# A gated recurrence and an ELU layer in one kernel: every engine's queue in a written-out order, and 53 products of zeros in place of 20

## The chip, the cores and the metric

The kernel runs on one core of a Trainium2 chip. The core has five engines with a queue each: TensorE (PE in the profile, its weight loads PEld), VectorE (DVE), ScalarE (ACT), GpSimd (POOL) and SyncE (SP, which here only issues DMAs). An engine works through its queue in order and waits on semaphores for the others. The metric is the device time in microseconds, the median of several runs.

## The reference, cut to what matters

```
sig = 1 / (1 + exp(-f_logit));  f = lower_bound + (1 - lower_bound) * sig     # (2, 6080, 256)
h[t] = f[t] * h[t-1] + (1 - f[t]) * x[t]                                      # a scan over 6080 steps
h1 = h.reshape(12160, 256) @ w_in                                             # w_in 256 x 2048
g  = where(h1 > 0, h1, exp(min(h1, 0)) - 1)                                   # ELU
out = g @ w_out                                                               # w_out 2048 x 256
```

All values are 32-bit floats.

## The kernel before, in words

The 6080 steps are cut into 12 pages (`SIZES`: 512, 448, then ten of 512). A page holds four tiles y of 128 channels by 512 steps: two halves of the channels (k) for two batches (t). The 2048 hidden columns are cut into eight quads of 2 x 128 columns, so the kernel runs through 96 quads (`NQ`).

To keep the precision, an operand is split into a high part that TensorE's fast format holds and the low rest, and a product becomes three: high by high, low by high, high by low. ScalarE's copy makes the high part, a subtraction on VectorE or POOL the low one (`operand`, `halves`, `split`). Only the first quad (`NATIVE = 1`) multiplies in plain 32-bit floats, which needs no splitting; each of its products takes four passes. The first 12 quads (`plain_quad`) multiply directly; later ones (`quad`) use seven products of sums and differences in place of eight (M1 to M7), and one quad a page from page 3 on is "wide" and does the same for the second matrix.

The weights come as 64-bit floats and are cut down to 32 bits on the chip: `conv` is an Abs on ScalarE (L855), a clamp (L903 on VectorE, L910 on POOL), a mask (L916) and two merging steps (L924). The scan of a page is `chain`: for each batch t, a tanh on ScalarE over f (L855), a scaling of it by the per-channel constants fa and fb (L851), a fused step on VectorE that forms (f - 1) * x (L1068) and the scan itself on VectorE (L1077). fa and fb are made on VectorE (L1464) from `lower_bound`, which ScalarE's queue loads by a DMA (L1460). The ELU of a tile is an exponential and a ReLU on ScalarE (L855) and a VectorE step (L1189). The second matrix's products (L1236) add up in PSUM; at the end of a page they are copied out and stored.

Ahead of the first real product TensorE runs products of a zero tile by itself (`idle`, L1448, 256 columns each). They write a PSUM tile that nobody reads.

No loop issues these instructions. Every operation is put into a plan, `Plan.add(engine, cost, want, fn, reads, writes, ...)`, and gets the next number. `Plan.order()` then simulates the engines with the given costs, always takes the operation that can start first (among near ties the one with the lowest `want`), and returns the order in which the program issues them. `SHIFT` moves the `want`, the earliest start or the patience of single operations. An operation with `other` may go to POOL in place of VectorE or the other way round, and products of zeros are dropped when they find no room (`latest`). Instructions of VectorE that touch SBUF alone (`lock`) and all of POOL's are chained: where two neighbours in the issued order are on different engines, the second waits for the first.

The numbers of the first operations, counted along the calls, are used below: 0 the zero tile's memset (POOL), 1 to 60 the products of zeros, 61 the load of `lower_bound`, 62 and 63 fb and fa, 64 to 71 the eight loads of page 0 (for t, for k: f then x, 256 KB each), 72 to 74 the first weight tile in three parts, 75 to 79 and 80 to 84 the `conv` of its parts 0 and 1, 85 to 92 the `chain` of t=0 (tanh 85, 86; scaling 87, 88; fused step 89, 90; scan 91, 92), 93 to 100 that of t=1 in the same way, 101 to 105 the `conv` of part 2. Of the later ones: 121 to 124 are the second weight tile's conv, 130 and 131 the high and the low half of it, 111 the low part of one y, 204, 210, 216 and 222 the last ELU step of the first quad's four tiles.

In the old order TensorE's queue begins with 19 products of zeros and has a 20th behind the first quad's second product. ScalarE's queue begins 61, 75, 80, 85, 87, 93; VectorE's 62, 63, 76, 77, 78, 79, 81, 82, 83, 84, 89, 91, 97, 99, 98, 102, 100, 103, 104, 90, 105, 92, 210, 222, 121; SP's 72, 73, 64, 71, 68, 65, 69, 70, 74.

Of the kernel before, what the change touches and what calls it, by code (L numbers as in the profile page):

```python
# [13 lines left out]
B, S, D, DFF = 2, 6080, 256, 2048  # L14
# [48 lines left out]
SHIFT = {  # L63
# [513 lines left out]
def stage(p):  # L577

    return str(p) if p <= WIDE_FROM else "e" if p == NP - 1 else "s"
# [1029 lines left out]
```

## Time and profile before

| | |
|---|---|
| time, median of 3 runs | 996.96 us (995.84 to 997.40) |
| span of the profiled execution | 995.6 us |
| its own time | not listed apart from the span; the median lies 1.4 us above it |
| TensorE | busy 984.9 us, 99% |
| weight loads | 813.9 us, 82% |
| VectorE | 763.5 us, 77% |
| ScalarE | 806.0 us, 81% |
| POOL | 423.3 us, 43% |
| DMA | 46.5 MB, 47 GB/s over the span |

A row of a timeline names its start, its duration, the engine, the line of the program, the operation, what it writes and reads and how many were merged; in square brackets stands the time for which the engine was idle before it, and what ended that. Ends of matmuls are modelled and overlap the next start.

### The profile page before, as it was taken

What the parts mean: (1) busy time and instruction counts of PE and PEld (TensorE: products, weight loads), DVE (VectorE), ACT (ScalarE), POOL (GpSimd) and SP (SyncE); (2) the same over time, 40 slices, a digit from 0 to 9 for tenths busy, and PEclk for the clock granted to TensorE, in tenths of its full rate; (3) what the DMA queues carried; (4) which work ended last, traced back from release to release, by engine and by line L of the source; (5) the groups of instructions that cost most, each with busy time, mean ns of one, the idle gap of its engine ahead of it and who ended that gap; (6) DMA issues with size and microseconds to landing.
All of it is one profiled execution on the core that took longest, in us unless ns stands there. A gap on an engine that the chain in (4) does not pass through costs nothing.

```text
span 995.6 us, 11936 instructions
## 1 busy us (share of the span) xinstructions
PE 984.9 (99%) x4333; PEld 813.9 (82%) x4333; DVE 763.5 (77%) x1005; ACT 806.0 (81%) x1138; POOL 423.3 (43%) x260
## 2 busy tenths in 40 slices
PE   7999999999999999999999999999999999999998
PEld 4788899888888878888888888888888888888886
DVE  7989788887888588687778678768868767867665
ACT  6899787976898698888879779878888887977764
POOL 0221414345525735634632742661563463274422
PEclk8999999999999999999999999999999999999999
DMA  6331121000020030010101102102001010100101
GB/s 211 128 122 38 69 101 43 37 1 1 22 106 1 1 126 8 36 67 18 43 23 62 43 1 85 43 1 86 5 38 64 23 43 20 66 0 1 43 1 43
DMA packets 10427, 46.51 MB, mean 47 GB/s; under 512 B 1280, under 2 KB 1280, under 8 KB 7808
## 3 DMA queue, kind: packets, MB, share of 16 engines
q1 hardware_dynamic: 10224, 45.75, 12.6%
q8 instruction: 34, 0.56, 0.2%
q14 instruction: 25, 0.20, 0.1%
q10 hardware_dynamic: 144, 0.00, 0.0%
HBM read 33.29 MB, written 12.45 MB: 46 GB/s over the span
## 4 chain that ended last, share of the span: by engine, by line
PE 97%; ACT 1%; DVE 1%; DMA 0%; issue 0%; SPq 0%; DVEq 0%
PE o L1236 51%; PE hv L1149 17%; PE hz L1149 17%; PE hx L1149 6%; DMA gh<-fx 0%; ACT e L855 0%; PE h(_188 L1134 0%; PE h(_205 L1134 0%; PE h(_195 L1134 0%; PE h(_202 L1134 0%; PE h(_263 L1149 0%; DVE v L924 0%; PE h(_304 L1149 0%; PE h(_336 L1149 0%; PE h(_350 L1149 0%
## 5 line engine op out<-in xcount | busy, mean ns | idle before, releaser
L838 POOL TENSOR_TENSOR gl<-hs,gh 128x1024 fp32r<-128x1024 f32 (+1 forms) x71 | 170.0, 2396 | 263.3 <-DVE y L1077 83.5
L855 ACT ACTIVATE e<-e 128x512 f32<-128x512 f32 (+3 forms) x278 | 208.0, 756 | 6.2
L1236 PE MATMUL o<-gh,woL 128*128 128x512 f32 (+1 forms) x706 | 208.9, 387 | 0.0
L1236 PE MATMUL o<-gl,woH 128*128 128x512 f32 (+1 forms) x706 | 204.8, 387 | 0.0
L1236 PE MATMUL o<-gh,woH 128*128 128x512 f32 (+1 forms) x706 | 204.3, 387 | 0.1
L1149 PE MATMUL hv<-yo,wiH 128*128 128x512 f32 (+1 forms) x504 | 190.0, 388 | 0.0
L1149 PE MATMUL hz<-yo,wiH 128*128 128x512 f32 (+1 forms) x504 | 188.8, 388 | 0.0
L1236 PEld LDWEIGHTS o<-gh,woH 128*128 128x128 f32 x706 | 132.4, 188 | 26.5 <-DVE v L838 0.5
L1236 PEld LDWEIGHTS o<-gh,woL 128*128 128x128 f32 x706 | 132.5, 188 | 26.4 <-ACT gh L849 0.3
L1236 PEld LDWEIGHTS o<-gl,woH 128*128 128x128 f32 x706 | 132.5, 188 | 26.2
L849 ACT CAST gh<-hs 128x1024 fp32r<-128x1024 f32 (+1 forms) x95 | 98.7, 1040 | 30.8 <-PE o L1236 22.6
L1189 DVE SCALAR_TENSOR_TENSOR hs<-hs,e 128x1024 f32<-128x1024 f32 (+1 forms) x84 | 101.9, 1213 | 20.0 <-POOL yo L838 9.3
L1149 PEld LDWEIGHTS hv<-yo,wiH 128*128 128x128 f32 x504 | 94.6, 188 | 19.8
L1149 PEld LDWEIGHTS hz<-yo,wiH 128*128 128x128 f32 x504 | 94.6, 188 | 19.4
L849 ACT CAST gh<-g 128x1024 fp32r<-128x1024 f32 (+1 forms) x80 | 83.2, 1040 | 26.3 <-DVE g L1189 18.1
L838 POOL TENSOR_TENSOR ys<-y 128x512 f32<-128x512 f32 (+1 forms) x52 | 66.7, 1292 | 77.3 <-DVE y L1077 36.1
L1149 PE MATMUL hz<-yo,wiL 128*128 128x512 f32 (+1 forms) x252 | 97.8, 388 | 0.0
L1149 PE MATMUL hv<-yo,wiL 128*128 128x512 f32 (+1 forms) x252 | 97.8, 388 | 0.0
L855 ACT ACTIVATE e<-hs 128x1024 f32<-128x1024 f32 (+1 forms) x84 | 88.5, 1054 | 11.4 <-DVE hs L838 9.2
L838 DVE TENSOR_TENSOR q<-q,hv 128x512 f32<-128x512 f32 (+1 forms) x84 | 57.0, 679 | 43.8 <-PE hv L1149 36.8
L838 DVE TENSOR_TENSOR gl<-g,gh 128x1024 fp32r<-128x1024 f32 (+1 forms) x58 | 70.2, 1210 | 24.9 <-POOL ys L838 8.8
L838 DVE TENSOR_TENSOR hs<-q,hv 128x512 f32<-128x512 f32 (+1 forms) x84 | 57.3, 682 | 32.0 <-PE hv L1149 25.2
(380 smaller groups left out, 1596.2 us busy)
## 6 DMA issues: line engine op xcount, KB each, us to landing
raw<-fx SPq DMA_DIRECT2D x20, 1024.0 KB, 4.6
out_t<-v SPq DMA_DIRECT2D x22, 512.0 KB, 2.9
raw<-w SPq DMA_DIRECT2D x15, 512.0 KB, 4.6
raw<-fx SPq DMA_DIRECT2D x2, 896.0 KB, 4.3
gh<-fx SPq DMA_DIRECT2D x4, 256.0 KB, 6.1
gl<-fx SPq DMA_DIRECT2D x4, 256.0 KB, 4.9
out_t<-v SPq DMA_DIRECT2D x2, 448.0 KB, 2.5
raw<-w SPq DMA_DIRECT2D x2, 256.0 KB, 3.1
```

The costliest lines, as they stand in the source:

```text
L838: return e, cost, lambda: engines[e].tensor_tensor(out=out_(), in0=in0(), in1=in1(), op=op)
L849: nc.scalar.copy(out=out_(), in_=in_())
L855: nc.scalar.activation(out=out_(), in_=in_(), func=func, **args)
L1149: nc.tensor.matmul(out=hb(q, b), lhsT=(wiH if m == "h" else wiL)[:, i, wi], rhs=T[kind, p, name], start=(start and j == 0), stop=(j == len ...
L1189: lambda: nc.vector.scalar_tensor_tensor(out=gt(), in0=src(), scalar=0.0, in1=et(), op0=ALU.max, op1=ALU.subtract,), reads=src_names + [e] ...
L1236: nc.tensor.matmul(out=accs[p, e, t], lhsT=lhsT, rhs=rhs, start=(c == 1), stop=(c == total(p, e, t)), skip_group_check=True,)
```

## The change

`SHIFT` goes, and with it the planner's simulation. In its place stands `ORDER`, a string of 4408 tokens: the numbers of the operations in the order in which they are issued. A `~` behind a number takes the operation's other engine.

```diff
-SHIFT = {
-    '00.L00.0': 6.99, '00.L01.0': 0.21, '00.L10.0': -3.16, '00.L11.0': 5.87, '00.M00.0': -0.25,
...
+ORDER = (
+    " 73 0 31 7 80 26 61 72 64 14 81 75 30 62 82 63 68 65 76 83 85 77 87 93 95 84 78 79 70 69 74 71"
+    " 94 96 89 91 6 40 97 99 17 12 3 28 1 8 25 29 50 23 21 38 18 16 27 101 4 48 43 9 19 5 66 67 13"
+    " 20 47 44 22 51 86 88 49 52 114 98 102 100 118 33 53 42 15 32 39 36 24 45 34 37 2 120 112 35"
+    " 90 103 46 11 10 212 200 41 92 119 104 206 218 207 208 209 219 220 221 210 105 121 122 222 110"
+    " 106 123 124 135 134 201 213 214 211 111 223 130 215 131 108 202 216 107 113 109 136 203 137"
...
+    " 4403 4404 4405 4409 4334 4406 4393 4407 4410 4408 4411 4413 4412 4414"
+)
     def order(self):
...
+        order, done = [], set()
+        for token in ORDER.split():
+            i = int(token.rstrip("~"))
+            o = self.ops[i]
+            assert o["deps"] <= done and i not in done
+            if token.endswith("~"):
+                o.update(eng=o["other"][0], cost=o["other"][1], fn=o["other"][2], lock=True)
+            order.append(i)
+            done.add(i)
+        assert all(i in done or o["spare"] for i, o in enumerate(self.ops))
+        return order
```

Only the order within each engine's queue, and between VectorE's and POOL's locked instructions, has an effect. Read by engine, the new queues begin:

- TensorE: 52 products of zeros, 212, 200 (the two products of the first y), one product of zeros, 206, 218 (second y), 207, 219 (third), 201, 213 (fourth), 211, 223.
- ScalarE: 80, 61, 75, 85, 87, 93, 95, 94, 96, 101, 86, 88, 114, 120.
- VectorE: 81, 62, 82, 63, 76, 83, 77, 84, 78, 79, 89, 91, 97, 99, 98, 102, 100, 90, 103, 92, 104, 210, 105, 121, 122, 222, 123, 124, 111, 131.
- SP: 73, 72, 64, 68, 65, 70, 69, 74, 71, 66, 67.

All 4355 real operations are in both orders. 127 of them change between VectorE and POOL: of the splits of hs 71 are on POOL before and 43 after, of the weight sums 12 before and 34 after. Each of the 12 pages has an order of its own; before, pages 4 to 10 shared one set of shifts. The costs in `act_cost`, `pool_cost`, `pe_cost` and of the loads and scans change too, but nothing reads them any more.

## Rows read from the trace of the kernel before

**Rows 1.** The page, part 1: busy us (share of span) and instructions by engine.
```profile
PE 984.9 (99%) x4333; PEld 813.9 (82%) x4333; DVE 763.5 (77%) x1005; ACT 806.0 (81%) x1138; POOL 423.3 (43%) x260
```
**Rows 2.** Windows of the start: length, busy us by engine, granted clock, DMA, GB/s.
```profile
8.00:9.00 1.00, 0.00 (x0) 0.00 (x0) 0.90 (x2) 0.75 (x1) 0.00 (x0) 0.88 1.05 373
...
15.00:16.00 1.00, 1.00 (x2) 0.30 (x2) 0.57 (x1) 0.91 (x2) 0.00 (x0) 0.70 0.00 0
```
**Rows 3.** Windows by stage, same columns (PE, PEld, DVE, ACT, POOL).
```profile
25.00:45.00 20.00, 20.00 (x81) 14.93 (x81) 18.82 (x26) 17.78 (x29) 4.53 (x4) 1.00 0.36 112
45.00:340.00 295.00, 295.00 (x1341) 251.47 (x1340) 237.46 (x333) 243.24 (x367) 119.98 (x83) 1.00 0.13 49
...
345.00:371.00 26.00, 25.77 (x111) 20.34 (x110) 21.32 (x29) 23.60 (x33) 9.63 (x4) 1.00 0.33 122
```
**Rows 4.** Waits of TensorE's weight loads: us in total, times, longest.
```profile
PEld o L1236 <- ACT raw L849: 0.6, 1, 0.6
...
PEld o L1236 <- ACT v L849: 0.2, 1, 0.2
```
**Rows 5.** Timeline of the first 25 us, all engines.
```profile
0.73 0.41 ACTq L1460 DMA_DIRECT2D lb_sb<-lb  x1
...
1.20 4.36 PE L1448 MATMUL hzeros<-zeros 128*128 128x256 f32 x19 [1.20 <-POOL zeros L1439]
...
3.71 0.43 ACT L855 ACTIVATE v<-raw 128x256 f32<-128x256 f32 x1 [1.26 <-DMA raw<-w]
3.94 0.17 DVE L1464 TENSOR_SCALAR fb<-lb_sb 128x2 f32<-128x2 f32 x1 [3.94 <-DMA lb_sb<-lb]
4.01 0.16 DVE L1464 TENSOR_SCALAR fa<-lb_sb 128x2 f32<-128x2 f32 x1
4.26 0.29 DVE L903 TENSOR_SCALAR v<-v 128x256 f32<-128x256 f32 x1
...
6.37 0.88 DVE L924 SCALAR_TENSOR_TENSOR v<-raw,v 128x256 int32<-128x256 int32 x2
...
8.06 0.69 DVE L1068 SCALAR_TENSOR_TENSOR gh<-gh 128x512 f32<-128x512 f32 x1 [0.81 <-DMA gh<-fx]
8.79 1.23 DVE L1077 TENSOR_TENSOR_SCAN y<-gh 128x512 f32<-128x512 f32 x1
...
10.16 2.04 PE L1134 MATMUL h(_188<-y,v 128*128 128x512 f32 x2 [4.60 <-DVE y L1077]
...
15.43 0.69 DVE L1068 SCALAR_TENSOR_TENSOR gh<-gh 128x512 f32<-128x512 f32 x1 [0.47 <-ACT gh L851]
...
16.64 1.22 DVE L1077 TENSOR_TENSOR_SCAN y<-gh 128x512 f32<-128x512 f32 x1
...
18.19 1.02 PE L1134 MATMUL h(_188<-y,v 128*128 128x512 f32 x2
...
18.82 0.69 DVE L1189 SCALAR_TENSOR_TENSOR g<-h(_205,e 128x512 f32<-128x512 f32 x1 [0.96 <-ACT e L855]
...
19.05 1.02 PE L1134 MATMUL h(_195<-y,v 128*128 128x512 f32 x2
...
24.77 0.50 PE L1149 MATMUL h(_263<-yo,wiL 128*128 128x512 f32 x1 [0.42 <-DVE wiL L838]
```
**Rows 6.** DMA issues: count, KB each, us from issue to landing (second row: 3.5 to 4.0).
```profile
lb_sb<-lb ACTq DMA_DIRECT2D x1, 1.0 KB, 3.2
...
gl<-fx SPq DMA_DIRECT2D x2, 256.0 KB, 5.3
...
out_t<-v SPq DMA_DIRECT2D x2, 448.0 KB, 2.5
```
**Rows 7.** Groups by line and form, POOL and VectorE: busy us, mean ns.
```profile
L838 POOL TENSOR_TENSOR gl<-hs,gh 128x1024 fp32r<-128x1024 f32 x67 | 161.5, 2411 | 251.4 <-DVE y L1077 83.5 <-ACT gh L849 52.1 <-DVE raw L838 34.1
...
L838 DVE TENSOR_TENSOR gl<-hs,gh 128x1024 fp32r<-128x1024 f32 x20 | 24.4, 1219 | 1.6 <-ACT gh L849 1.6
```
**Rows 8.** Timeline of the tail.
```profile
991.50 0.58 ACT L849 COPY v<-o 128x512 f32<-128x512 f32 x1 [4.64 <-PE o L1236]
```

More of the change, by code (lines that the diff above doesn't have):

```diff
@@ L60 @@
 COPIES = {"M2": 2, "M5": 3}
-SHIFT = {
[510 rows of a table removed]
-}
+ORDER = (
[232 rows of a table added]
+)
 def stage(p):
-    return str(p) if p <= WIDE_FROM else "e" if p == NP - 1 else "s"
+    return "abcdefghijkl"[p]
 def wide(q):
@@ L593 @@
 class Plan:
-    LAG = 0.12
-    PATIENCE = 0.155
-    DRAIN = 0.17
-    TIE = 0.05
-    LINED = ()
     def __init__(self, pools):
@@ L645, in add @@
         deps.discard(i)
-        used = set(reads) | set(writes) | set(adds)
         self.ops.append(dict(
-            eng=eng, cost=cost, want=want + SHIFT.get(key, 0.0), fn=fn, key=key, deps=deps, used=used, takes=list(takes),
-            lock=lock, soonest=max(soonest, self.gate) + SHIFT.get(key + "@", 0.0),
-            latest=latest, other=other, patience=self.PATIENCE + SHIFT.get(key + "~", 0.0),
+            eng=eng, cost=cost, want=want, fn=fn, key=key, deps=deps, takes=list(takes), lock=lock,
@@ L651, in add @@
+            soonest=max(soonest, self.gate), spare=latest is not None, other=other,
         ))
     def order(self):
-        ops = self.ops
-        n = len(ops)
-        after = [[] for _ in range(n)]
-        missing = [len(o["deps"]) for o in ops]
-        for i, o in enumerate(ops):
-            for d in o["deps"]:
-                after[d].append(i)
-        users = {}
-        home = {}
-        for o in ops:
-            for pool, name in o["takes"]:
-                home[name] = pool
@@ L666, in order @@
-        for i, o in enumerate(ops):
-            for b in o["used"]:
-                if b in home:
-                    users[b] = users.get(b, 0) + 1
-        slots = {p: [0.0] * k for p, k in self.pools.items()}
-        asks = {}
-        for o in ops:
-            if o["latest"] is None:
-                for name in [name for pool, name in o["takes"] if pool in self.LINED]:
-                    asks[name] = min(asks.get(name, float("inf")), o["want"])
-        lines = {p: [] for p in self.pools}
@@ L678, in order @@
-        for name in sorted(asks, key=asks.get):
-            lines[home[name]].append(name)
-        for p in lines:
-            lines[p].reverse()
-        held, ends = set(), {}
-        ready = [o["soonest"] for o in ops]
-        def engines(o):
-            return [o["eng"], o["other"][0]] if o["other"] else [o["eng"]]
-        waiting = {}
-        for i, o in enumerate(ops):
-            for e in engines(o):
-                waiting.setdefault(e, set())
-                if not missing[i]:
-                    waiting[e].add(i)
@@ L694, in order @@
-        free = {e: 0.0 for e in waiting}
-        locked, holder = 0.0, None
-        dropped = set()
-        start = [0.0] * n
-        done = [0.0] * n
-        left = n
-        while left:
-            best = None
-            for e, mine in waiting.items():
-                for i in [
-                    i for i in mine
-                    if ops[i]["latest"] is not None and max(ready[i], free[e]) > ops[i]["latest"]
-                ]:
-                    mine.discard(i)
-                    dropped.add(i)
-                    left -= 1
-                able = []
-                for i in mine:
-                    o = ops[i]
-                    t = asked = max(ready[i] + (o["patience"] if e != o["eng"] else 0.0), free[e])
-                    lock = o["lock"] or e == "POOL"
-                    if lock:
-                        t = max(t, locked + (self.LAG if e != holder else 0.0))
-                    for pool, name in o["takes"]:
-                        if name not in held:
-                            turn = name not in asks or lines[pool][-1] == name
-                            t = max(t, min(slots[pool])) if slots[pool] and turn else float("inf")
-                    if t < float("inf"):
-                        able.append((t, o["want"], i, asked if lock else t))
-                if not able:
-                    continue
-                first = min(able)[0]
-                pick = min((k for k in able if k[0] < first + self.TIE), key=lambda k: k[1:3])
-                if (best is None or (pick[0], pick[3]) < (best[0], best[3])):
-                    best = (*pick, e)
-            if best is None:
-                break
-            t, _, i, _, e = best
-            o = ops[i]
-            if e != o["eng"]:
-                o.update(eng=e, cost=o["other"][1], fn=o["other"][2], lock=True)
-            for pool, name in o["takes"]:
-                if name not in held:
-                    slots[pool].remove(min(slots[pool]))
-                    held.add(name)
-                    if name in asks:
-                        lines[pool].pop()
-            start[i] = t
-            free[e] = t + o["cost"]
-            done[i] = t + o["cost"] + (self.DRAIN if e == "PE" else 2.8 if e == "SP" else 0.0)
-            if o["lock"] or e == "POOL":
-                locked, holder = t + o["cost"], e
-            for mine in waiting.values():
-                mine.discard(i)
-            left -= 1
-            for b in o["used"]:
-                if b in home:
-                    users[b] -= 1
-                    ends[b] = max(ends.get(b, 0.0), done[i] + self.LAG)
-                    if not users[b]:
-                        slots[home[b]].append(ends[b])
-            for j in after[i]:
-                missing[j] -= 1
-                lag = 0.0 if ops[j]["eng"] == e and e != "PE" else self.LAG
-                if ops[j]["eng"] == "PE" and e == "PE":
-                    lag = -self.DRAIN
-                ready[j] = max(ready[j], done[i] + lag)
-                if not missing[j]:
-                    for x in engines(ops[j]):
-                        waiting[x].add(j)
@@ L764, in order @@
-        self.start, self.done = start, done
-        assert not left
-        return sorted(set(range(n)) - dropped, key=lambda i: (start[i], i))
-def act_cost(n, ptr=False):
-    return 0.19 + n / 1200 + (0.19 if ptr else 0.0)
+        order, done = [], set()
[7 more added lines that the diff above has]
+            done.add(i)
@@ L773, in dve_cost, with act_cost @@
+        assert all(i in done or o["spare"] for i, o in enumerate(self.ops))
+        return order
+def act_cost(n, ptr=False, psum=False):
+    return (0.16 if psum else 0.2) + n / 1200 + (0.18 if ptr else 0.0)
 def dve_cost(n, fast=False):
@@ L777, in pool_cost @@
 def pool_cost(n, two=True):
-    return 0.2 + n * 2.15e-3 if two else 0.1 + n * 1.0e-3
+    return 0.2 + n * 2.15e-3 if two else 0.02 + n * 1.0e-3
 def pe_cost(n):
-    return (n + 32) / 2400
+    return 0.2027 if n == 448 else (n + 32.2) / 2400
 @with_exitstack
@@ L855, in fn @@
                 nc.scalar.activation(out=out_(), in_=in_(), func=func, **args)
-        plan.add("ACT", act_cost(n, ptr is not None), want, fn, **kw)
+        psum = any(isinstance(r, tuple) and r[0] in ("h", "acc") for r in kw["reads"]) if "reads" in kw else False
+        plan.add("ACT", act_cost(n, ptr is not None, psum), want, fn, **kw)
     w32 = w.bitcast(I32)
@@ L876, in load_w @@
         plan.add(
-            "SP", 1.28 * (hi - lo) / (2 * D), want, fn, writes=[("raw", i, part)],
+            "SP", 1.25 if hi - lo == 2 * D else 0.73, want, fn, writes=[("raw", i, part)],
             reads=[("raw", i)], takes=[("raw", ("raw", i))], soonest=0.75,
@@ L1037, in load_fx @@
         plan.add(
-            "SP", 1.28 * len(ks) * (0.5 if a is not None else 1), want, fn, reads=[name],
+            "SP", 1.25 * len(ks) if a is None else 0.73, want, fn, reads=[name],
             writes=[("fxp", p, t, k, z) for k in ks for z in (range(2) if a is None else [a])],
@@ L1080, in scan @@
                 )
-            plan.add("DVE", 0.18 + n / 480, want + 1.5, scan,
+            plan.add("DVE", 0.21 + n / 480, want + 1.5, scan,
                      reads=rd([k]) + wr([k], (0, 1)), writes=[("y", a)], lock=True)
```

735 rows, old and new, of tables (ORDER, SHIFT) are left out of this document.

## The prediction

> **What bounds the kernel now.** I read the page first: TensorE is busy 99% of the span [rows 1], and the chain of waits runs on it nearly throughout. A reader must not stop there, because a busy matmul can still run at half clock; so next come the granted clock and the busy time by stage. From 45 to 340 us TensorE is busy for all 295.00 us, at full clock [rows 3]; the later stages look the same. The only stretch after the start in which TensorE lost anything is 345 to 371 us, where it sat idle for 0.23 us [rows 3] and its weight loads waited 1.6 us in four groups (0.6, 0.5, 0.3, 0.2; the first and the last stand in [rows 4]). The rest of what can be won lies in the first 25 us. There TensorE runs 19 products of zeros from 1.20 to 5.56, stands still until 10.16, and starts the real work then [rows 5]; the granted clock is at its upper level, 2.4 GHz, until the slice 8 to 9 us, whose mean of 0.88 puts the fall to 1.2 GHz at 8.76, and back up in the slice 15 to 16, whose mean of 0.70 puts the rise at 15.6 [rows 2]. The number of real products and their shapes do not change, so the change can move only four things: when real work starts, the half clock behind that start, waits of TensorE, and the tail.
>
> The ceiling of a gain follows. The first real product starts at 10.16. The wait for data just ahead of it that another order could shorten is the 0.81 us that VectorE idles for x before 8.06 [rows 5]. Half clock from 10.16 to about 15.6 costs half of that stretch, 2.7 us. Waits up to 24.77 (0.42 us there, and shorter ones ahead of it) are estimated at 1.3 us, and the four late ones at most 1.6 us. Together about 6.4 us, 0.6% of the time.
>
> **The change part by part.**
>
> *The tail.* In both orders the last product into the t=0 accumulators (4405) is followed by five groups of two products for t=1, and then by the same VectorE and ScalarE evacuations and the store. 991.50 to the end of the span stays [rows 8]. Cost 0, and the two VectorE evacuations for t=0 still fit beside the five groups.
>
> *The loads of page 0.* SP's old order is w0 part 0, w0 part 1, f(t0,k0), x(t1,k1), f(t1,k0), x(t0,k0). The new one is w0 part 1, w0 part 0, f(t0,k0), f(t1,k0), x(t0,k0). So x(t0,k0), for which VectorE waited until 8.06 [rows 5], is fifth, not sixth. Each load is 256 KB, and the successive waits show about 0.7 us a load; it lands near 7.3. By itself this would start the first real product 0.7 us earlier.
>
> *The load of lower_bound.* This is the edit that decides. In the old order op 61, the load of `lb`, is the first thing in ScalarE's queue: issued at 0.73, and VectorE's first instruction, fb, starts on its landing at 3.94, 3.2 us later [rows 5, 6]. In the new order ScalarE's queue begins 80, 61, 75. Op 80 is the Abs of w0 part 1 and waits for a weight load; the Abs that stands first among ScalarE's arithmetic today starts at 3.71, ended by just such a landing [rows 5]. A queue runs in order, so the load of `lb` is issued behind that wait, near 3.75. With the 3.2 us of today it lands at 7.0.
>
> VectorE's new order is 81, 62, 82, 63, 76, 83, 77, 84, 78, 79, then 89 and 91. Op 62 is fb, so behind 62 wait all the rest of both weight conversions, and the chain that makes y. Today fb and fa take from 3.94 to 4.17 and the eight conversion steps run from 4.26 to 7.25 [rows 5]. Of these, 81 (the 0.29 us row) still runs before the wait. So op 89 starts at 7.0 + 0.23 + 2.70 = 9.9, against 8.06. From 89 to the end of the first scan is 8.06 to 10.02 today, 1.96 us; the first y stands at 11.86, and the first product starts at 12.0 against 10.16: 1.85 us later. ScalarE's own step that needs fb and fa (87, 0.81 us) would be done at 8.5 and hides beside this. The earlier x wins nothing, since 9.9 is later than its landing.
>
> The 3.2 us were measured with the other queue just starting; under a full queue the two 256 KB loads issued at 3.5 and 4.0 took 5.3 us from issue to landing [rows 6]. The lower bound is the Abs itself plus nothing (no load lands before it is issued): 3.75. The upper bound is 3.75 + 5.3, as those two, 9.05. I take 3.2 because it is the same transfer of 1 KB, on a queue of its own.
>
> The Trainium skill, page "DMA: Bandwidth & Descriptors", says under "Queues, rings and completion order" that each DMA engine takes turns between the queues it has work for, so a small load on a queue of its own would not stand behind SP's backlog; no row here has `lb` loaded under such a backlog. Under "Anatomy of one DMA" the same page gives about 2.0 us for setup and completion (fitted on another issue path); the row of 3.2 us disagrees, and by 2.0 the landing would be an estimated 5.75 and the first product at 10.75.
>
> *VectorE behind that.* Today 89's start to the end of the fourth scan is 8.06 to 17.86, 9.8 us. In it are 0.47 us of idle (ahead of the 15.43 instruction) and two conversion steps of about 0.6 us (104, 105) that the new order puts behind that scan. New: 9.9 + 9.8 - 0.47 - 1.2 = 18.0, so the last y of the page is only 0.15 us late: the better order takes back most of what the late `lb` costs. To the end of op 131, the low half of the second weight tile, on which TensorE waited until 24.77 [rows 5], the new queue has ten instructions, together 6.0 us by their spacings today. If the g of the first quad is there when its turn comes, 131 ends at 24.0 and TensorE goes on at 24.15: 0.6 us earlier than 24.77. From there TensorE has no wait until 45 us (20.00 us busy of 20.00 from 25 on, [rows 3]), and what VectorE must still deliver (the second tile's low half, due 0.5 us before its use) just holds. So the whole rest of the kernel shifts by what this point shifts.
>
> *The zeros.* 52 products of zeros stand ahead of the first real one in TensorE's queue and one behind the second. 19 take 4.36 us at the slow rate, 0.23 us each [rows 5]; at full clock a product of half the width of the usual one (0.22 us, 295.00 us over 1341, [rows 3]) is estimated at 0.12. Since the clock falls at 8.76 it must have risen before, and the rate of the 19 shows that it rose near their end; from 5.4 on the other 33 take 0.12 each and end at 9.3. They would have met a first product at 9.4; one at 12.0 leaves 2.7 us of idle. Today the clock fell about 3.2 us after the last zero [rows 2, 5]. So two cases. (a) It stays up: the first eight products are bound by the scans, the last ends at 19.9, g comes in time, and the sum is -0.6. (b) It falls at about 12.2. Then the two products of the first y take 1.7 us each and not 0.86 (two records, 18.19 to 19.05 at full clock, [rows 5]). If it returns when these are done, the eight end at 20.8, op 210 waits 1.0 us for ScalarE's exponential, as it waits 0.96 today [rows 5], and 131 ends at 25.0: +0.35. If it returns 5.4 us after the first product, as today, one more product and part of the next run slow, and the sum is +1.2. Between these I take +0.8. Were all 52 slow, 52 x 0.23 would end at 13.2 and delay the start by 1.2. The Trainium skill, page "TensorE: Matmul & The Clock Gate" (Part 1), adds that the moment of change is not tied to the program's start and so differs between runs; no single run here can show that. I give (a) and (b) equal weight: +0.1.
>
> *The order behind 25 us.* 127 subtractions and sums change between VectorE and POOL, net one. Splits of hs go from 71 on POOL to 43, other ones the other way. A 1024-wide one takes 2.41 us on POOL and 1.22 on VectorE [rows 7], so POOL loses some 35 us and VectorE gains about 20, on engines with 57% and 23% to spare; hidden as long as each comes before TensorE's turn. Bounds for TensorE: all four late waits gone, -1.6; or waits of that kind (0.2 to 0.6 us each) in a few of the later pages, which today have none, +2.5. I take half of 1.0, the middle of 0.23 and 1.6 rounded up: -0.5.
>
> **Sum.** +0.1 - 0.5 = -0.4 us on the span of 995.6, so 995.2. The span lies 1.4 us under the median 996.96; with the same 1.4 the time is 996.6.
>
> **Rivals.**
> 1. *The load of `lb` does not hold VectorE up* (it lands by about 4.2, or its issue is not held). Then 89 starts at 7.3, the zeros meet the first product at 9.4, the clock stays up, and 131 ends near 22.0: -2.7 - 0.5, so 993.8. For it: everything else in the first queue orders fits a start at 9.4, the 52 zeros above all. Against it: op 80's wait stands ahead of 61 in one queue.
> 2. *The load lands sooner than today's.* The shortest transfer of the page, a store, takes 2.5 us [rows 6]; then it lands at 6.25, all that follows is 0.75 earlier, the idle shrinks and the clock stays up: -0.6 - 0.75 - 0.5, so 995.1. For it: this transfer is far smaller than that store; against: the 3.2 us of the same load. By the 2.0 us of the page named above it would be 994.6.
> 3. *The load lands late*, as the large ones do, at 9.05. First product at 14.1, idle 4.8 us, the clock falls for certain and the first four products run at half rate; 131's successor starts at 28.0 against 24.77, +3.2 - 0.5: 999.7, slower. It decides from a landing of about 8.7. For it: the 5.3 us in [rows 6]; against: those loads stand behind one another in one queue, and `lb` does not.
> 4. *New waits in the later pages*, +2.5 with the start as forecast: 999.4. For it: each page now has an order of its own with no slack shown; against: TensorE has none of them for 295 us today, and POOL gets lighter.
>
> **Chances.** Forecast 0.58 (995.3 to 998.3 its own range); rival 1 0.10, rival 2 0.10, rival 3 0.12, rival 4 0.10. The range is 993.7 to 999.0: it takes in rivals 1 and 2 and leaves out most of 3 and 4. What a measurement here can tell from no change is 0.2%, 2.0 us: faster is below 994.97 and slower above 998.95. Faster: rival 1, half of rival 2 and a little of the forecast, 0.20. Slower: most of 3 and 4, 0.18. Same: 0.62.
>
> **What would show it.** ScalarE's issue of lb_sb near 3.75, and VectorE's fb idle until about 7.0; the first real product near 12.0; zeros ending near 9.3 with 0.12 us each after the rise; the granted clock with a dip from about 12 or none; the wait for wiL ending between 24.1 and 25.1; no waits of weight loads between 345 and 371. A first product before 10.2, or fb before 6, makes the prediction wrong on its main step; waits of TensorE after 45 us of more than 2 us together make it wrong on the other.

## The result and the profile after

The changed kernel takes 1004.88 us (median of 4 runs, 1004.22 to 1006.17) against 996.81 us for the kernel before beside it: ratio 1.0081, 95% interval 1.0068 to 1.0094. It is 8.1 us slower, outside the range given. The profiled span went from 995.6 to 1003.3 us, 7.7 us more.

The page, part 1, after (beside [rows 1]):

```profile
PE 994.2 (99%) x4366; PEld 813.5 (81%) x4366; DVE 782.8 (78%) x1004; ACT 799.4 (80%) x1138; POOL 378.4 (38%) x261
```

TensorE is still 99% busy, and 9.3 us of busy time have been added: 33 more products of zeros (about 4 us, 1.20 to 9.40 below instead of 1.20 to 5.56), and something that this line can't show. POOL lost 45 us and VectorE gained 19, where about 35 and 20 were forecast. The start, from the timeline of the changed kernel (start, duration, engine, line, operation, in brackets the idle time before it and what ended it):

```profile
1.20 8.20 PE L1061 MATMUL hzeros<-zeros 128*128 128x256 f32 x52 [1.20 <-POOL zeros L1052]
...
3.60 0.38 ACTq L1073 DMA_DIRECT2D lb_sb<-lb  x1
...
8.78 0.17 DVE L1077 TENSOR_SCALAR fb<-lb_sb 128x2 f32<-128x2 f32 x1 [4.33 <-DMA lb_sb<-lb]
...
11.00 0.68 DVE L681 SCALAR_TENSOR_TENSOR gh<-gh 128x512 f32<-128x512 f32 x1
...
11.72 1.23 DVE L690 TENSOR_TENSOR_SCAN y<-gh 128x512 f32<-128x512 f32 x1
...
13.09 2.05 PE L747 MATMUL h(_270<-y,v 128*128 128x512 f32 x2 [3.69 <-DVE y L690]
...
14.93 1.92 PE L747 MATMUL h(_272<-y,v 128*128 128x512 f32 x2
```

Compare with [rows 5]. The load of `lower_bound` is issued at 3.60 and VectorE stands still for 4.33 us until it lands at 8.78, 5.2 us after its issue and not 3.2. The first real product comes at 13.09, not 10.16. TensorE has then been idle for 3.69 us since the last zero, and two products start 1.84 us before the next pair; at full clock it is 0.86 ([rows 5], 18.19 to 19.05). Three windows, in which the granted clock is the figure behind the POOL column:

```profile
11.00:12.00 1.00, 0.00 (x0) 0.00 (x0) 0.96 (x3) 1.00 (x2) 0.00 (x0) 0.98 1.07 430
12.00:13.00 1.00, 0.00 (x0) 0.00 (x0) 1.00 (x2) 0.97 (x3) 0.00 (x0) 0.50 1.01 410
18.00:19.00 1.00, 1.00 (x2) 0.35 (x2) 1.00 (x2) 0.00 (x0) 0.00 (x0) 0.61 0.00 0
```

A mean of 0.98 puts the fall from 2.4 to 1.2 GHz at 11.96, before the first product; 0.61 puts the rise at 18.8. So the 33 additional zeros bought nothing here: half clock for as long behind the first product as before, 3 us later. At the product that the kernel before starts at its 44 us TensorE is 2.8 us behind it. (Ahead of the first rise the traces have no record of the clock, and the column shows 1.00 there too. The distance of the zeros tells it: about 0.21 us at half clock, 0.12 at full.)

The rest is lost bit by bit behind the start, and the busy columns hide it. The stages after (first row to be held against [rows 3]), then those of the kernel before that do not stand there:

```profile
45.00:340.00 295.00, 295.00 (x1336) 249.32 (x1335) 244.41 (x323) 241.55 (x368) 105.09 (x92) 1.00 0.16 53
340.00:550.00 210.00, 209.97 (x920) 171.08 (x919) 169.02 (x209) 173.81 (x238) 79.19 (x49) 1.00 0.12 38
550.00:750.00 200.00, 200.00 (x877) 162.88 (x876) 155.10 (x193) 160.64 (x223) 86.64 (x55) 1.00 0.12 40
750.00:980.00 230.00, 230.00 (x1010) 188.23 (x1009) 171.68 (x217) 180.78 (x247) 93.29 (x55) 1.00 0.08 28
```

```profile
340.00:550.00 210.00, 209.77 (x923) 172.42 (x922) 164.30 (x206) 176.35 (x239) 93.17 (x53) 1.00 0.12 46
550.00:750.00 200.00, 200.00 (x884) 165.42 (x883) 150.13 (x191) 164.62 (x226) 101.40 (x61) 1.00 0.10 37
750.00:980.00 230.00, 230.00 (x1016) 190.21 (x1015) 168.00 (x212) 181.76 (x247) 100.52 (x56) 1.00 0.07 28
```

"Busy 295.00 of 295.00" stands in both kernels. But the counts of products in the same time fell: 1341 to 1336, 923 to 920, 884 to 877, 1016 to 1010. That is 21 of 4164 in 935 us, at 0.2245 us each 4.7 us. Laying the n-th product of one trace beside that of the other gives the same: +2.8 us at 44 us, +3.5 at 215, +4.1 at 315, +3.6 at 400, +5.2 at 596, +7.3 at 896, +7.8 at the end; the last accumulator's copy starts at 999.29 and no longer at 991.50 [rows 8]. So **the start costs 2.8 us and the pages 5.0**, spread over all of them.

About half of that is in the waits of the weight loads behind 45 us (us in total, times, longest), the first six groups of many:

```profile
PEld o L849 <- ACT gh L461: 2.4, 12, 0.3
PEld o L849 <- POOL gl L450: 1.8, 6, 0.4
PEld hz L762 <- DVE q L450: 1.7, 8, 0.3
PEld o L849 <- ACT v L461: 1.3, 7, 0.2
PEld hz L762 <- DVE g L802: 1.1, 5, 0.3
PEld hv L762 <- DVE g L802: 0.9, 4, 0.3
```

In these names gh and gl are the high and the low half of an ELU result, q the copy of a quad's first product, hv and hz the product tiles that are added to it, hs the second pair of hidden tiles, e the exponential, g the ELU result, o an accumulator of the second matrix and v here mostly the tile into which it is copied out.

Before there were four such waits, 1.6 us in all. Now the view, which lists waits of more than 0.15 us, has 54, together 12.3 us, most of 0.2 to 0.3 us, on all three engines. A weight load that starts late costs less than its wait, since it normally runs beside the product ahead: around these 54 the starts of the products are 4.2 us further apart than usual. One of them, with TensorE's neighbours, in the second page (448 steps):

```profile
165.33 0.36 PE L762 MATMUL hv<-yo,wiL 128*128 128x448 f32 x1
...
165.53 0.37 PE L762 MATMUL hv<-yo,wiH 128*128 128x448 f32 x1
165.84 0.30 PEld L849 LDWEIGHTS o<-gl,woH 128*128 128x128 f32 x2 [0.32 <-POOL gl L450]
165.84 0.67 PE L849 MATMUL o<-gl,woH 128*128 128x448 f32 x2
...
166.35 0.57 PE L849 MATMUL o<-gh,woH 128*128 128x448 f32 x2
```

Products of this size start 0.20 us apart. POOL's gl ends at 165.79, and the product that reads it starts 0.31 after its neighbour; the pair then takes 0.51 until the next pair instead of 0.40. So a weight load that waited 0.32 us costs 0.21, in two steps: its own product comes 0.1 us late, and so does the next one, whose weight load could start only 0.11 us behind the first. The modelled end of the product ahead covers the gap, so PE shows no idle time.

The starts of all products behind 44 us show the other half. Usually they are 0.227 us apart, 0.203 in the second page. 39 of the distances are longer by more than 0.05 us, 3.6 us together; in the kernel before there are 6, 1.0 us together. Another 445 are longer by 0.004 to 0.05 us, 3.0 us together; before, 156 and 0.9. These small delays stand in no view, and no run here shows what causes them.

### The profile page after: what moved, and what is told of

Same layout as the page of the kernel before. It is cut to its first block, busy times and chain, and to the rows that moved or that the text cites. A ratio compares the mean times of both kernels' runs of the same rounds, so it can differ in the third digit from the quotient of the medians.

```text
span 1003.3 us, 12016 instructions
## 1 busy us (share of the span) xinstructions
PE 994.2 (99%) x4366; PEld 813.5 (81%) x4366; DVE 782.8 (78%) x1004; ACT 799.4 (80%) x1138; POOL 378.4 (38%) x261
## 3 DMA queue, kind: packets, MB, share of 16 engines
q1 hardware_dynamic: 10224, 45.75, 13.4%
## 4 chain that ended last, share of the span: by engine, by line
PE 98%; DMA 1%; DVE 0%; ACT 0%; SPq 0%; issue 0%
PE o L849 52%; PE hz L762 17%; PE hv L762 17%; PE hx L762 6%; DMA gh<-fx 1%; PE h(_279 L747 0%; PE h(_270 L747 0%; PE h(_272 L747 0%; PE h(_342 L762 0%; PE h(_376 L762 0%; PE h(_338 L762 0%; PE h(_453 L762 0%; PE h(_403 L762 0%; PE h(_518 L762 0%; PE h(_354 L762 0%; PE h(_938 L762 0%
## 5 line engine op out<-in xcount | busy, mean ns | idle before, releaser
L467 ACT ACTIVATE e<-e 128x512 f32<-128x512 f32 (+3 forms) x278 | 205.8, 755 | 4.5
L849 PE MATMUL o<-gh,woH 128*128 128x512 f32 (+1 forms) x706 | 208.7, 388 | 0.0
L762 PE MATMUL hv<-yo,wiH 128*128 128x512 f32 (+1 forms) x504 | 193.4, 390 | 0.0
L762 PE MATMUL hz<-yo,wiH 128*128 128x512 f32 (+1 forms) x504 | 193.0, 390 | 0.0
L450 POOL TENSOR_TENSOR gl<-hs,gh 128x1024 fp32r<-128x1024 f32 (+1 forms) x45 | 107.0, 2379 | 141.4 <-ACT gh L461 50.0
L450 POOL TENSOR_TENSOR ys<-y 128x512 f32<-128x512 f32 (+1 forms) x49 | 63.3, 1295 | 140.2 <-DVE y L690 78.5
L450 POOL TENSOR_TENSOR yo<-ys,yo 128x512 fp32r<-128x512 f32 (+1 forms) x49 | 62.9, 1288 | 52.9 <-DVE gl L450 20.8
```

Of the source, the lines that this page charges most:

```text
L450: return e, cost, lambda: engines[e].tensor_tensor(out=out_(), in0=in0(), in1=in1(), op=op)
L467: nc.scalar.activation(out=out_(), in_=in_(), func=func, **args)
L762: nc.tensor.matmul(out=hb(q, b), lhsT=(wiH if m == "h" else wiL)[:, i, wi], rhs=T[kind, p, name], start=(start and j == 0), stop=(j == len ...
L849: nc.tensor.matmul(out=accs[p, e, t], lhsT=lhsT, rhs=rhs, start=(c == 1), stop=(c == total(p, e, t)), skip_group_check=True,)
```

## The experiments

"Ahead" and "behind" below are read as above, at TensorE's same product in the trace of the kernel before: at its 44 us, and at the end.

**1. The load alone.** Op 61 goes first in ScalarE's queue again; everything else as in the changed kernel.

```diff
-    " 73 0 31 7 80 26 61 72 64 14 81 ...
+    " 61 73 0 31 7 80 26 72 64 14 81 ...
```

> The changed kernel with one token moved: the load of lower_bound stands first in ScalarE's queue again, all else as changed. Theory A (two causes that add up: the late load costs the start, and the new order of the pages loses 5.0 us by itself): first real product near 9.4 in place of 13.09, start 2.7 us ahead of the kernel before, pages lose 5.0 as in the changed kernel, 999.2 us. Theory B (the waits in the pages are a consequence of the late start): pages lose nothing, 994.2 us. Theory C (the load costs only the 2.8 us by which the changed kernel stands late at 30 us, the rest of the new start is worth nothing): 1001.9 us.

Measured 999.61 us (999.36 to 999.90), ratio 1.0028 [1.0017, 1.0039]. The load lands 3.1 us after its issue, the products of zeros and the real ones meet, and the first pairs start 0.86 us apart, at full clock:

```profile
1.21 8.59 PE L1050 MATMUL hzeros<-zeros 128*128 128x256 f32 x52 [1.21 <-POOL zeros L1041]
9.63 1.02 PE L736 MATMUL h(_270<-y,v 128*128 128x512 f32 x2
10.49 1.02 PE L736 MATMUL h(_272<-y,v 128*128 128x512 f32 x2
```

This is rival 1's start: 3.4 us ahead of the kernel before at 44 us, where 2.7 was forecast. At the end it is 2.3 us behind: the pages lose 5.7 us, with a start that is early. That is theory A. The place of this one load is worth 5.3 us in the changed order (1004.88 against 999.61).

**2 and 3. The two halves apart.** The orders are cut where TensorE comes to the sixth quad. First the new start (61 first) with the old order behind it; then the old start with the new order behind it.

```diff
 ORDER, run 2:  new order, 61 first, up to the sixth quad | old order from there
 ORDER, run 3:  old order up to the sixth quad | new order from there
```

> Every operation that the kernel before issues ahead of its sixth quad's first product stands in the order of the changed kernel (load of lower_bound first, 52 zeros ahead, one behind); everything after that in the order of the kernel before. Theory A: the start gains 2.7 us and the pages lose nothing, 994.2 us, less than both kernels. Theory C: 996.9 us. If the join itself makes TensorE wait, up to 998.

> The other way round: what the changed kernel issues ahead of its sixth quad's first product stands in the order of the kernel before (load of lower_bound first, 19 zeros and a 20th), the rest in the changed order. Theory A: start as before, pages lose 5.0 us, 1001.9 us. Theory B (the waits follow from the late start): 996.9 us.

Run 3: 1002.24 us, ratio 1.0051 [1.0038, 1.0064], theory A: the pages' loss comes with the new order whatever the start (1.2 us ahead at 44 us, 3.7 behind at the end, 4.9 lost). Run 2: 996.08 us, ratio 0.9992 [0.9983, 1.0001], a miss: it loses 2 of its 3.2 us of lead at once, at two waits just behind the cut. That the old order meets there a TensorE which is earlier than it was made for is my reading; no run tests it:

```profile
70.17 0.73 PE L838 MATMUL o<-gl,woH 128*128 128x512 f32 x2 [0.41 <-DVE gl L439]
72.60 0.47 PE L751 MATMUL h(_762<-yo,wiH 128*128 128x512 f32 x1 [0.77 <-DVE e L791]
```

**4. The zeros alone.** The old order with 52 products of zeros ahead.

```diff
-    20 products of zeros, where the planner found room
+    1 to 52 behind the memset of the zero tile (op 0)
```

> The kernel before with 52 products of zeros ahead of the first real one and none behind; nothing else moved. If they keep the clock up: no half clock from 10.16 to 15.6, the first g 0.9 us and the next one 0.5 us earlier, the wait for the second weight tile's low half ends near 23.5, time 995.7 us. If the scans bind that stretch anyway: 996.9 us. If the zeros run into the first product: the start later by up to 1.2 us, 998.

Measured 996.18 us, ratio 0.9995 [0.9985, 1.0004]: not told from no change. In the trace it is 1.3 us ahead at 44 us and stays so; the first pair of products goes from 10.27 to 11.20, full clock. But this lead can't be put down to the zeros. Runs 3 and 7 begin with the old order's 19 zeros and are 1.2 us ahead at 44 us too, because in their executions the clock rose at 13.4 us and not, as in the trace of the kernel before, at 15.6. What the traces do show of the zeros: in all eight with 52 zeros that run up to the real work (runs 1, 2, 4 to 6, 9 to 11) the clock rises between 4.3 and 7.4 us and does not fall again before the last product; in all five with the old order's 19 ahead (before, runs 3, 7, 8, 12) it is at half when the first product starts.

**5. Slack given back to TensorE.** In run 1's trace 98 groups of products (a group is what one operation of the plan issues) behind 45 us start less than 0.3 us after their operand is ready (before: 26). For 87 of them products that stood behind were pulled ahead.

```diff
 TensorE's queue, 87 times:
-    tight group, products ready for longer
+    products ready for longer (0.4 us of them), tight group
```

> The changed order with the load of lower_bound first (999.61 us), and in TensorE's queue behind 45 us 87 of the 98 groups of products that started less than 0.3 us after their operand was there are moved one to three groups later, behind groups whose operands had been there for 0.6 us or more. Nothing else moves. Theory D (the pages lose because groups stand right at the landing of their operands, so that each small delay stops TensorE): of the 5.7 us that the pages lose at most 2.5 are left, 996.5 us or less. Theory E (the changed choice of engines makes operands late as a whole, so that a wait moved away comes back at the next group): 998.6 to 999.6 us.

Measured 1002.65 us, ratio 1.0057 [1.0044, 1.0069], 3.0 us worse than run 1: both theories failed. The groups that start less than 0.3 us after their operand fell from 98 to 52, but the listed waits became fewer and longer: 44 of 14.8 us together in place of 53 of 12.1 (for v of VectorE 2.7 us in 7, for gh of ScalarE 3.1 in 9, up to 0.7 each). A likely cause, not tested: what TensorE does later reaches ScalarE and VectorE later, and they answer later.

**6. A later cut.** As run 2, but cut at the twelfth quad.

```diff
 ORDER:  new order, 61 first, up to the twelfth quad | old order from there
```

> As the run with the new start and the old pages, but joined later: the new order (load of lower_bound first) up to the twelfth quad's first product, the old order behind it. If the lead of 3.4 us was lost there because the old order has VectorE form the weight sums and conversions of that stretch, which the new one gives to POOL: lead of 3.2 us kept, 993.7 us. If any join to the old pages loses it: 995.9 us or more.

Measured 995.45 us (994.74 to 996.20), ratio 0.9984 [0.9975, 0.9993]: faster than both kernels, by 1.3 us. The forecast was missed again: of 2.9 us of lead 1.7 go behind the cut. About 0.8 us of it goes at 115 to 117 us, where weight loads wait 0.4 us for VectorE's hs and 0.6 for ScalarE's v. ScalarE is full there, 5.00 of 5.00 us, but that alone is no cause, since the kernel before has 4.97 in the same window and loses nothing. The rest goes up to 174 us, over the second page, whose products start some nanoseconds further apart:

```profile
104.00:115.00 11.00, 11.00 (x54) 9.65 (x52) 6.63 (x12) 10.20 (x21) 8.66 (x11) 1.00 0.00 1
115.00:120.00 5.00, 4.79 (x23) 3.89 (x23) 3.32 (x7) 5.00 (x12) 0.30 (x1) 1.00 0.26 105
```

**7. The engines alone.** The old order with the new order's 127 choices between VectorE and POOL.

```diff
 ORDER:  old order, with `~` at the operations that have it in the new one
```

> The order of the kernel before, with the changed kernel's choice between VectorE and POOL for the 127 operations that change engine. Theory E (the choice costs the pages their time): 5 us or more above the kernel before, 1002 us. Theory D (their place in TensorE's queue does): within 1.5 us of the kernel before, 998.4 us at most.

Measured 1027.14 us, ratio 1.0303 [1.0289, 1.0317]. The choices can't be carried over without their order, so this run can't decide between D and E. The largest wait is for a POOL split:

```profile
PEld o L837 <- POOL gl L438: 9.6, 12, 1.6
```

**8. The late load alone.** The old order with op 61 behind ScalarE's first Abs.

```diff
-    61 0 62 63 72 73 64 71 68 65 75 69 76 80 ...
+    0 72 73 64 71 68 65 75 61 62 63 69 76 80 ...
```

> The order of the kernel before with the load of lower_bound issued behind ScalarE's first Abs; nothing else. If it lands 5.2 us after its issue, as in the changed kernel: near 8.8, the first scan's step at 12.0, first product at 14.0, 3.5 to 4 us slower, 1000.6 us. If it lands 3.2 us after its issue, as where it is first: near 7.0, 2 us slower, 998.9 us.

Measured 1000.67 us, ratio 1.0036 [1.0023, 1.0048]. As expected: this one edit costs 3.9 us. Its load takes as long as in the changed kernel:

```profile
3.54 0.39 ACTq L1061 DMA_DIRECT2D lb_sb<-lb  x1
...
8.87 0.17 DVE L1065 TENSOR_SCALAR fb<-lb_sb 128x2 f32<-128x2 f32 x1 [8.87 <-DMA lb_sb<-lb]
...
14.00 2.04 PE L735 MATMUL h(_188<-y,v 128*128 128x512 f32 x2 [8.38 <-DVE y L678]
```

**9 to 12. Which engine is late in the pages.** Run 1's order with work taken from ScalarE, from VectorE, from both; and the old order with both cuts. The orders stay.

```diff
 run 9, 11, 12 (elu):
-        act(width, want + 0.6, et, et, func=ACTF.Relu, bias=1.0, scale=-1.0, writes=[e])
+        act(width, want + 0.6, lambda: et()[:, :width // 8], lambda: et()[:, :width // 8], func=ACTF.Relu, ...)
 run 10, 11, 12 (quad):
-            tt("DVE", n, o("q" + bk, off), lambda: T[qn], lambda: T[qn], lambda bk=bk: hb(q, bk),
+            tt("DVE", n, o("q" + bk, off), lambda: T[qn][:, :n // 8], lambda: T[qn][:, :n // 8], lambda bk=bk: hb(q, bk)[:, :n // 8],
```

> The new order with the load of lb first on ScalarE (999.6 us), and the second step of every exponential, the in-place ReLU on e (178 of 630 ns on 512 columns and 80 of 1059 ns on 1024), done on the first eighth of the columns only; the other columns keep the bare exponential, so that part of the computation is left out. ScalarE becomes some 130 us lighter of 799. The order itself stays. Behind the start, the new pages lose about 5.7 us in this kernel against the old ones. Theory F (the new order puts ScalarE's answers a few tenths of a us behind TensorE's turn): most of it vanishes, 994 to 996 us. Theory G (VectorE's answers): little vanishes, 998.5 to 999.6. Theory H (both lie in one loop of TensorE, ScalarE, VectorE and back, and anything that shortens the loop helps): about half, 996 to 998. Theory I (POOL, or TensorE's own order): nothing, 999 or more.

> The new order with lb first, and the two sums of a quad into q (q + hv, q + hz: 160 of 683 ns on 512 columns) done on the first eighth of the columns only; the other columns of q stay what ScalarE copied, so that part of the computation is left out. VectorE becomes some 80 us lighter of 783, and the PSUM tiles that the two sums read come free earlier. Theory F (ScalarE): 998.5 to 999.6. Theory G (VectorE): 994 to 996. Theory H (one loop): 996 to 998. Theory I (POOL or TensorE's own order): 999 or more.

> Both cuts at once: the ReLU on e and the two sums into q on the first eighth of the columns, so both parts of the computation are left out. Theories F, G and H all expect that no wait of TensorE behind the start is left: the start as with lb first (2 to 3 us ahead of the kernel before) and no loss behind it, 993 to 995 us. Theory I: 998 or more.

> The kernel before with both cuts of the run ahead of it (the ReLU on e and the two sums into q on the first eighth of the columns). Here the planner, which knows nothing of the cuts, keeps the old order. All theories expect the same: what the old order waits for behind the start is at most 1.6 us, and its start gains at most 0.5 us, so 994.8 to 996.8. If it falls below 993, the cuts win time by another way than by waits, and the three runs ahead of it say less.

| run | time, us | ratio | shift at 44 us | at the end | lost between |
|---|---|---|---|---|---|
| 1, no cut | 999.61 | 1.0028 [1.0017, 1.0039] | -3.4 | +2.3 | 5.7 |
| 9, ScalarE light | 996.93 | 0.9998 [0.9989, 1.0007] | -3.6 | -0.7 | 2.9 |
| 10, VectorE light | 997.32 | 1.0002 [0.9993, 1.0010] | -3.3 | -0.1 | 3.2 |
| 11, both light | 994.32 | 0.9973 [0.9962, 0.9983] | -3.2 | -2.7 | 0.4 |
| 12, old order, both light | 995.67 | 0.9986 [0.9977, 0.9995] | -1.7 | -2.1 | -0.4 |

All four numbers are those of theory H, and F, G and I, each as the only cause, are out: each cut takes about half of the pages' loss (2.8 and 2.5 us), both together 5.3 of 5.7. Run 12 shows that the cuts by themselves give the old order only 0.4 us behind the start. POOL's part can't be read from this sum, since with ScalarE and VectorE lighter POOL's operands come earlier too: the waits for its gl fall from 1.8 us in run 1 to 1.0 in run 11. The waits behind 45 us of runs 1, 9, 10 and 11 in turn:

```profile
PEld o L838 <- ACT gh L450: 2.3, 11, 0.3
PEld hz L751 <- DVE q L439: 1.8, 8, 0.3
PEld o L838 <- POOL gl L439: 1.8, 6, 0.4
```

```profile
PEld hz L751 <- DVE q L439: 1.6, 7, 0.3
...
PEld o L838 <- ACT gh L450: 1.0, 5, 0.2
```

```profile
PEld o L838 <- ACT gh L450: 2.4, 10, 0.4
```

```profile
PEld o L838 <- POOL gl L439: 1.0, 3, 0.4
PEld o L838 <- ACT v L450: 0.8, 4, 0.2
PEld o L838 <- ACT gh L450: 0.7, 3, 0.3
```

Each cut clears above all the waits for its own engine: with ScalarE light those for its gh fall from 2.3 us in run 1 to 1.0 and those for VectorE's q into hz stay (1.8, 1.6); with VectorE light the q is gone from the list and gh stays at 2.4. In all the view lists 53 waits and 12.1 us in run 1, then 32 and 7.3, 29 and 7.0, 12 and 2.9. But a cut helps the other engine too: with ScalarE light the waits for VectorE's g fall from 2.0 us to 1.1, with VectorE light those for ScalarE's v from 1.3 to 0.8. So two engines are each late by a little, in part at places of their own and in part through each other, as in H's loop. The small delays that no view lists go with them: 502 in run 1, then 350, 388 and 206.

## Why the prediction was wrong

**The steps that held.** The issue of `lb` behind the Abs (3.75 forecast, 3.60), VectorE held by fb, the end of the zeros (9.3, 9.40), the 2.1 us from op 89 to the first product (11.00 to 13.09), POOL lighter and VectorE heavier, the tail. The rise of the clock near 5.4 us held too (5.14), but not by the reading that gave it: the 19 zeros of [rows 5] are about 0.21 us apart to the last one, so their rate shows only that the clock had not risen by 5.2. In run 1 rival 1's start came true, larger than its 2.7 us.

**The step that failed first: "with the 3.2 us of today it lands at 7.0".** It landed at 8.78, 5.2 us after its issue. I had the upper bound of 5.3 from the large loads [rows 6] and took the nearest row, that of the same transfer, though the state of the DMA engines was not the same. The prediction's own rival 3 was right, with its condition (a landing behind 8.7), its price (+3.2, measured +2.8) and its sign. The chain behind fb was 0.7 us shorter than I had it (2.22 us from fb to op 89, not 2.93): the first product came at 13.09 where rival 3 had 14.1. The clock then fell at 11.96, my case (b). The two cases were drawn from a single execution, and that this one came out as (b) is in part luck: the old start had the rise at 15.6 in one execution and at 13.4 in two others (runs 3 and 7). Against the start of run 3 the changed kernel is 4.0 us behind at 44 us, not 2.8. Run 8 shows the edit alone: +3.9 us on the time.

**The second: "the order behind 25 us ... -0.5".** Measured +5.0, twice the upper bound of +2.5 and of the other sign. The bound rested on "waits of that kind (0.2 to 0.6 us each) in a few of the later pages". They came in all the pages, 54 of them, on all three engines, and they are only about half of the loss; the other half is in small delays that the step did not have at all. The argument that POOL gets lighter and the others have share to spare was an average; what decides is by how much each operand is early, and the busy shares don't tell that: 98 groups start less than 0.3 us after their operand in run 1, 26 in the kernel before. Run 3 shows this loss without the late start, run 1 with an early one, runs 9 to 11 that a lighter ScalarE and VectorE take away 5.3 of its 5.7 us. The gain that the step counted on did come: of the late waits of [rows 4] 1.6 us became 0.6 in the same stretch of work (349 to 375 us after), and the shift falls there from 4.1 to 3.6 us, the forecast -0.5. It drowned in the rest.

**Sum.** 2.8 + 5.0 = 7.8 against 7.7 on the span. Rivals 3 and 4 came true at once, the latter at twice its price, and I had left no room for that: I treated them as alternatives and cut the range at 999.0, though they are independent, and even their sum by my own prices, 2.7 + 2.5 + 0.5 = 5.7, would have been 1002.7. (Rival 4's own 999.4 leaves out the +0.1 of the start that it names; with it the sum is 999.6.)

What stays open: why ScalarE and VectorE are late at just these places, which part of the new order (the choices of engine or the queues) makes them so, and what the small delays are. The one attempt to mend it from TensorE's queue alone, run 5, failed. A mend of ScalarE's and VectorE's own orders was not tried.

## What to carry to other kernels

When an edit moves a small load behind a wait, price it by what else the DMA engines carry at its new time, not by its old duration. On an engine that is 99% busy with modelled ends, count products per window, lay their starts beside those of the kernel before and list the waits of weight loads: busy time can't show a loss of half a per cent made of delays of 0.1 us and less. Before a lead at the start is put down to an edit, look at whether the clock rose at the same moment in both traces. And an order for five engines is one thing: a stretch of it put beside another's lost more than half of its lead behind the seam (runs 2 and 6), and its engine choices in another order cost 3% (run 7).

## What the runs showed of the hardware

- **A 1 KB load took 2 us longer beside full DMA engines.** 3.2 us in the kernel before, with the DMA engines at a share of 0.62 in its flight; 5.2 in the changed one at 1.01, and 5.3 in run 8 at 0.98; 3.0 to 3.3 wherever it was issued first. The windows of the flight, before and after (the last two figures: share and GB/s):

```profile
0.70:3.90 3.20, 2.70 (x12) 2.70 (x13) 0.00 (x0) 1.47 (x2) 0.42 (x1) 1.00 0.62 182
```

```profile
3.60:8.80 5.20, 5.20 (x40) 5.20 (x40) 0.31 (x2) 1.50 (x3) 0.00 (x0) 1.00 1.01 328
```

  A queue of its own did not spare the load the backlog. The Trainium skill, page "DMA: Bandwidth & Descriptors", section "Queues, rings and completion order", has the engines take turns between queues; read as "the small load does not wait", that rule fails here by 2.0 us. The section "Latency and other measured facts" of the same page of the Trainium skill gives the access to the chip's memory as 0.2 us on average and 2 us at high load; the difference, an estimated 1.8 us, fits the 2.0 measured. The trace splits the flight in part. The load's packets are a queue of their own (q10, 144 packets): the first one starts 1.6 us after the issue before (at 2.32) and 3.3 us after it in the changed kernel (6.86), and from the first to the last it is 1.0 and 1.6 us. So 1.7 of the 2.0 us pass before the first packet and most of the rest between packets. Whether the load waits there for its turn or for the memory stays open.
- **A weight load's wait costs TensorE less than it lasts.** The 54 waits of the changed kernel, 0.15 to 0.45 us each and 12.3 us together, made the distances between products 4.2 us longer: nearly nothing for a wait of 0.16 (at 526.07), 0.1 us for one of 0.26 (at 484.67), 0.21 for one of 0.32 (at 165.84).
- **The clock rises at another moment in another execution of the same start.** TensorE's queue begins alike in the kernel before and in runs 3 and 7; in the first the clock is up from 5.35 to 8.76 us and again from 15.6, in the others it rises at 13.4 and their TensorE is 1.2 us ahead at 44 us. The old order's pages passed on 1.2 to 1.4 us of three different leads (1.3, 3.2 and 2.9 us at 44 us in runs 4, 2 and 6), so against run 3's start next to nothing is left of them; by their times runs 2 and 4 can't be told from no change, and only run 6 is faster, by 1.3 us.
